# Seven groups of twelve small loads in the load queue of a decode kernel

## The chip, the cores and the metric

The kernel runs on one core of a Trainium2 chip. The metric is the time of one execution in device microseconds; the median of six runs stands for the kernel. A profiled execution gives the trace; it is one execution more, with its own time.

## What is computed

One token passes two pairs of layers, with the same weights in both pairs. The first of a pair is attention over a window of the last 4,096 positions of a cache (32 heads of 192), the second a gated feed-forward layer. Cut to what matters:

```python
def _A_ref(x, k_cache, v_cache, wq, wo):          # x: 1 x 1 x 640
    q = (x @ wq) split into 32 heads of 192
    k, v = the last 4096 positions of k_cache, v_cache   # 32 x 4096 x 192 each
    p = softmax(q k^T * 192 ** -0.5)
    return (p v) @ wo
def _B_ref(x, w1, w3, w2):                         # hidden width 1536
    return (silu(x @ w1) * (x @ w3)) @ w2
x = x + _A_ref(layernorm(x), ...)
x = x + _B_ref(layernorm(x), ...)
x = x + _A_ref(layernorm(x), ...)
x = x + _B_ref(layernorm(x), ...)
```

All arrays are bf16. K and V of the window are about 50 MB each and don't fit on the chip, so nearly all of them are read twice.

## The kernel before, in words

The 32 heads are worked on in four blocks of eight, and a block in four pieces of two heads (`z` = 0 to 3). The K of a piece is one load of 3 MB into all 128 partitions, and so is its V. Layer 0 (the code's name for the first pair) takes the blocks in the order 0, 1, 2, 3 and layer 1 in the order 3, 2, 1, 0; most of block 3 stays on the chip between the layers.

All loads go into one large array `pg`, in which places are given out by hand: seven slots of 3 MB (`slot(0)` to `slot(6)`, counted over all partitions), an area `AUX` for weights, a working area, and `KEPT`, 24 groups of V columns that stay from the end of layer 0 to the first values stage of layer 1. The list of loads, with place and source, is written out ahead by calls of `plan`, `plan_k`, `plan_v` and `plan_cut`. `need(key)` takes the list in order and issues loads on SP's queue (`nc.sync.dma_start`, L111) up to the one that is wanted. So the order on SP's queue is the order of the plan, and only the waits on SP's queue decide when a load is issued: the wait for the readers of what stood in the place before (DVE transposes, PE matmuls), and the wait for a completion semaphore to come free. There are eight of these for the DMA, used in turn, so a load can also wait for the one issued eight before it. One other load, of the token `x` into `xb`, is issued on ACT's queue (L208).

The work on a block: DVE transposes each K in place, four instructions a piece (`k_transpose`, L337); PE computes the scores (`k_scores`, L345; in layer 1's first block two pieces at a time, `pair_scores`, L362); DVE and ACT do the softmax (`softmax_front`, `softmax_back`, L372 to L396); PE multiplies with V (`v_values`, L406); `combine` (L420 to L430) and `times_columns` (L438) put the heads together and multiply with the output weights. The steps of neighbouring blocks are interleaved: the K steps of the next block alternate with the V steps of this one (`steps = "k0 v0 k1 v1 k2 v2 k3 v3"`). In layer 1 the first block goes `v1 v2 v3 k0 v0 k1 k2 k3`, so the values of `v0`, which read `KEPT`, come after a K step. The feed-forward layer follows (`ffn_hidden`, `ffn_out`); the result is stored by SP (L520).

Of the kernel before, what the change touches and what calls it, by code (L numbers as in the profile page):

```python
# [35 lines left out]
KEPT = 14592  # L36
# [27 lines left out]
def kernel(  # L64
# [13 lines left out]
    nc = tc.nc  # L78
# [12 lines left out]
    pg = pages.tile([P, NPG], BF16, name="pg")  # L91

    wq_v = A_wq.rearrange("(p c) n -> p (c n)", c=NCH)
# [9 lines left out]
    def plan(key, at, n, src):  # L103
        queue.append((key, at, n, src))

    def need(key):
        while key not in place:
            k, at, n, src = queue.pop(0)
            for other, (a, m) in live.items():
                assert at + n <= a or a + m <= at, (k, other)  # L110
            nc.sync.dma_start(out=pg[:, at:at + n], in_=src)  # L111
            place[k] = live[k] = (at, n)
        at, n = place[key]
        return pg[:, at:at + n]

    def done(key):
        del live[key]

    def slot(s):
        return SLOT0 + s * SLOT  # L120

    def kv_src(cache, b, z, t0=0, nt=TP):
        off = ((HB * b + 2 * z) * SK + S0 + t0) * DH
        return bass.AP(cache.tensor, cache.offset + off, [[TP * DH, 64], [SK * DH, 2], [1, nt * DH]])

    def plan_k(layer, b, z, s):
        plan(("k", layer, b, z), slot(s), SLOT, kv_src(A_k_cache, b, z))
# [3 lines left out]
    def plan_v(layer, b, z, *places):  # L131
        t = 0
        keys = vkeys[layer, b, z] = []
        for at, nt in places:
            key = ("v", layer, b, z, t)
            if at is None:
                key = ("v", 0, b, z, t)
            else:
                plan(key, at, nt * DH, kv_src(A_v_cache, b, z, t, nt))
            keys.append(key)  # L140
            t += nt

    def cut_v(s):
        at, out_ = slot(s), []
        for nt in CUT_V:
            out_.append((at, nt))
            at += nt * DH
        return out_

    def plan_cut(key, width, cuts, src, at):  # L150
        x = 0
        for i, n in enumerate(cuts):
            plan(key + (i,), at[i] if isinstance(at, tuple) else at + x, n * width, src[:, x:x + n * width])
            x += n * width
# [7 lines left out]
    for i, (n, at) in enumerate(zip(CUT_Q0, (slot(0), slot(1), AUX))):  # L162
        plan(("wq", 0, i), at, n * H * DH, wq_v[:, x:x + n * H * DH])
        x += n * H * DH
    for z in range(NZ):
        plan_k(0, 0, z, 2 + z)
    for (b, ks, vs) in ((0, (6, 1, 3, 5), (0, 2, 4, 6)),
                        (1, (0, 2, 4, 6), (1, 3, 5, 0)),
                        (2, (1, 3, 5, 2), (2, 4, 6, 4))):
        for z in range(NZ):  # L170
            plan_k(0, b + 1, z, ks[z])
            plan_v(0, b, z, (slot(vs[z]), TP))
        plan_cut(("wo", 0, b), D, (12,), wo_v[b], AUX)
# [17 lines left out]
        vkeys[1, 3, z] = list(vkeys[0, 3, z])  # L191
    for (b, ks, vs) in ((2, (4, 1, 5, 6), (0, 3, 2, 4)),
                        (1, (0, 3, 2, 4), (1, 5, 6, 0))):
        for z in range(NZ):
            plan_k(1, b - 1, z, ks[z])
            plan_v(1, b, z, (slot(vs[z]), TP))
        if b == 2:
            plan_cut(("wo", 1, b), D, (12,), wo_v[b], AUX)
    for z, s in enumerate((1, 3, 5)):
        plan_v(1, 0, z, (slot(s), TP))  # L200
    plan_v(1, 0, 3, *cut_v(2))
    plan_cut(("wo", 1, 1), D, (12,), wo_v[1], AUX)
    plan_cut(("wo", 1, 0), D, CUT_WO, wo_v[0], slot(6))
    plan_ffn(1, (slot(4), slot(0), slot(1)))

    need(("wq", 0, 0))
    xb = cst.tile([P, NCH], BF16, name="xb")
    nc.scalar.dma_start(out=xb[:], in_=A_x[0, 0, :].rearrange("(p c) -> p c", c=NCH))  # L208
# [223 lines left out]
    def times_columns(keys, cuts, od, y_ps, first, last):  # L432
        ci = 0
        for key, n in zip(keys, cuts):
            w = need(key)
            for i in range(n):
                for c in range(NCH):
                    nc.tensor.matmul(y_ps[:, c:c + 1], lhsT=w[:, D * i + c:D * i + D:NCH], rhs=od[:, ci:ci + 1],  # L438
                                     start=(first and ci == 0 and c == 0), stop=(last and ci == 11),
                                     skip_group_check=True)  # L440
                ci += 1
            done(key)
# [9 lines left out]
    def ffn_hidden(layer, od):  # L452
        g_ps = ps_a.tile([P, 512], F32, tag="a", name="g_ps")
        c = 0
        for i, n in enumerate(CUT_1[layer]):
            w = need(("w1", layer, i))
            for cl in range(n):
                for j in range(4):
                    nc.tensor.matmul(g_ps[32 * j:32 * j + 32, 0:384], lhsT=xw[:, c, 3:35],
                                     rhs=_ap(w, 0, P, FF * cl + 3 * j, [[12, 128], [1, 3]]),  # L460
                                     start=(c == 0), stop=(c == NCH - 1), tile_position=(0, 32 * j))
                c += 1
            done(("w1", layer, i))
            if i == 0:
                st, rstd = statistics()
                nc.vector.tensor_scalar(out=xn[:], in0=xsq[:, 0:NCH], scalar1=st[:, 0:1], scalar2=rstd[:],
                                        op0=ALU.subtract, op1=ALU.mult)
# [6 lines left out]
        for i, n in enumerate(CUT_3[layer]):  # L474
            w = need(("w3", layer, i))
            for cl in range(n):
                for f in range(12):
                    nc.tensor.matmul(u_ps[:, f:f + 1], lhsT=w[:, FF * cl + f:FF * cl + FF:12],  # L478
                                     rhs=xn[:, c:c + 1], start=(c == 0 and f == 0), stop=(c == NCH - 1),
                                     skip_group_check=True)  # L480
                if c == 0:
                    for k in range(3):
                        nc.tensor.matmul(gt_ps[:, k, :], lhsT=g_sb[:, k:384:3], rhs=selm[:, 0, :], start=True, stop=True)
                    gt = gt_ps[:].rearrange("p k j -> p (k j)")
                    gs = sml.tile([P, 12], F32, tag="gs", name="gs")
                    nc.vector.tensor_scalar_mul(out=gs[:], in0=gt, scalar1=rstd[:])
                    ex = sml.tile([P, 12], F32, tag="ex", name="ex")
                    nc.scalar.activation(out=ex[:], in_=gs[:], func=ACTF.Exp, scale=-1.0)
                    nc.vector.tensor_scalar_add(out=ex[:], in0=ex[:], scalar1=1.0)
                    nc.vector.reciprocal(out=ex[:], in_=ex[:])  # L490
                    nc.vector.tensor_tensor(out=sg[:], in0=gs[:], in1=ex[:], op=ALU.mult)
                c += 1
            done(("w3", layer, i))
# [220 lines left out]
```

## Time and profile before

| | |
|---|---|
| median of 6 runs | 532.5 us (531.7 to 533.56) |
| profiled execution | 532.67 us, span 531.0 us |
| PE busy | 281.7 us, 53% of the span |
| DVE busy | 250.7 us, 47% |
| ACT, POOL busy | 38.1 us, 18.4 us |
| moved by DMA | 221.33 MB, mean 417 GB/s |
| loads issued by SP | 112, from 320 KB to 3 MB |

The span is that of the trace from the first instruction to the last; the execution's time has a little around it. A page of the profile gives busy time by engine, then 40 slices of the span with busy tenths of each engine and of the 16 DMA engines, the DMA queues (q1 is SP's), a chain of waits followed back from the last instruction, and groups of instructions and of DMA issues with their times. A busy share is an average; which engine bounds a stage is read from the slices and from who waits for whom.

### The profile page before, as it was taken

How to read it: one execution, taken by the hardware profiler on the slowest of the kernel's cores; microseconds unless marked ns; L12 is line 12 of the kernel's file. 1: busy time of each engine (PE TensorE's matmuls, PEld its weight loads, DVE VectorE, ACT ScalarE, POOL GpSimd, SP SyncE). 2: the span in 40 equal slices, each digit the busy share in tenths (PEclk: the TensorE clock that was granted, in tenths of full speed). 3: DMA queues.
4: the chain of work that ended last, by engine and by line, in shares of the span. 5: the costliest groups of instructions: out<-in, count | busy, mean ns of one | idle time of the engine just before them, and what ended most of it. 6: DMA issues, size and time to landing. Idle time of an engine off the chain costs nothing.

```text
span 531.0 us, 6794 instructions
## 1 busy us (share of the span) xinstructions
PE 281.7 (53%) x2978; PEld 121.9 (23%) x2978; DVE 250.7 (47%) x304; ACT 38.1 (7%) x93; POOL 18.4 (3%) x71
## 2 busy tenths in 40 slices
PE   1417755550754507836356864944784335845464
PEld 0201111110311103213135432211321122212143
DVE  1269974436484084654011228958465265453010
ACT  0000020000200020002000012002000020002000
POOL 6000000000000000000002040000000000000000
PEclk9998787775678758877665697877777757977555
DMA  8999999999999999999999999999999999999994
GB/s 356 422 434 439 420 439 424 434 424 435 431 425 429 431 433 427 435 421 436 418 383 404 364 399 426 431 433 430 433 429 427 431 430 435 425 433 427 418 409 195
DMA packets 16310, 221.33 MB, mean 417 GB/s; under 512 B 1944, under 2 KB 1944, under 8 KB 7704
## 3 DMA queue, kind: packets, MB, share of 16 engines
q1 hardware_dynamic: 16136, 220.90, 98.5%
q8 instruction: 23, 0.38, 0.3%
q14 instruction: 7, 0.06, 0.0%
q10 hardware_dynamic: 144, 0.00, 0.0%
HBM read 220.89 MB, written 0.00 MB: 416 GB/s over the span
## 4 chain that ended last, share of the span: by engine, by line
DMA 65%; PE 13%; DVE 12%; issue 6%; ACT 2%; SPq 0%; ACTq 0%; DVEq 0%
DMA pg<-in_A_k_cache_dram 47%; DVE pg L337 9%; DMA pg<-in_B_w_dram 7%; DMA pg<-in_A_v_cache_dram 7%; PE s_ps_176 L345 4%; PE s_ps_177 L345 3%; DMA pg<-in_A_wq_dram 2%; PE o_ps L406 2%; DMA xb<-in_A_x_dram 2%; PE y_ps L438 2%; PE s_ps_177 L362 2%; ACT pg L381 1%; DVE pg L384 1%; ACT pg L394 1%; DVE pg L329 0%
## 5 line engine op out<-in xcount | busy, mean ns | idle before, releaser
L337 DVE STREAM_TRANSPOSE pg<-pg 128x1536 uint32<-128x1536 uint32 x112 | 189.0, 1745 | 102.6 <-DMA pg<-in_A_k_cache_dram 102.6
L345 PE MATMUL s_ps_176<-pg 128*32 128x512 bf16 x384 | 87.1, 617 | 59.3 <-DVE pg L337 59.3
L345 PE MATMUL s_ps_177<-pg 128*32 128x512 bf16 x288 | 66.8, 625 | 52.5 <-DVE pg L337 50.1
L345 PEld LDWEIGHTS <-pg 128*32 128x32 bf16 x672 | 41.3, 117 | 209.9 <-issue 196.6
L406 PE MATMUL o_ps<-pg 128*16 128x384 bf16 (+1 forms) x1024 | 74.7, 377 | 25.6 <-DMA pg<-in_A_v_cache_dram 19.8
L406 PEld LDWEIGHTS <-pg 128*16 128x16 bf16 (+1 forms) x1024 | 30.4, 98 | 57.2 <-issue 40.6
L423 PE MATMUL ot_ps<-o_sb,pg 128*128 128x192 bf16 x16 | 3.5, 317 | 64.2 <-ACT o_sb L420 64.2
L438 PE MATMUL y_ps<-otd,pg 128*128 128x1 bf16 x540 | 23.3, 178 | 11.7 <-DVE otd L430 6.8
L438 PEld LDWEIGHTS <-pg 128*128 128x128 bf16 x540 | 23.1, 131 | 13.8 <-issue 8.0
L427 DVE SCALAR_TENSOR_TENSOR om<-ot_ps,rl,dsel 128x192 f32<-128x192 f32 x8 | 3.1, 387 | 37.5 <-PE ot_ps L423 37.5
L381 ACT ACTIVATE pg<-s_ps_176,pg 32x512 bf16<-32x512 f32 x8 | 6.6, 821 | 192.1 <-DVE pg L378 192.0
L381 ACT ACTIVATE pg<-s_ps_177,pg 32x512 bf16<-32x512 f32 (+1 forms) x8 | 6.6, 819 | 169.3 <-DVE pg L378 169.2
L223 POOL MEMSET pg<- 128x128 f32 (+2 forms) x7 | 1.5, 219 | 465.7 <-PE u_ps L478 276.7
L384 DVE STREAM_TRANSPOSE pg<-pg 128x1024 bf16<-128x1024 bf16 x8 | 10.0, 1245 | 15.6 <-ACT pg L381 15.6
L423 PEld LDWEIGHTS <-pg 128*128 128x128 bf16 x16 | 1.6, 100 | 67.8 <-issue 67.8
L415 DVE RECIPROCAL rl<-rl_ps 128x1 f32<-128x1 f32 x8 | 1.3, 169 | 29.7 <-PE rl_ps L413 29.7
L309 PE MATMUL q_ps<-pg,xw 128*32 128x384 bf16 x80 | 7.0, 521 | 15.8 <-DVE xw L219 11.2
L394 ACT COPY pg<-pg 32x256 bf16<-32x256 bf16 (+1 forms) x36 | 14.3, 396 | 7.6 <-DVE pg L384 7.0
L225 POOL TENSOR_SCALAR_AFFINE_SELECT pg<-pg 128x128 f32<-128x128 f32 (+2 forms) x41 | 14.0, 342 | 3.0 <-POOL pg L223 0.3
L362 PE MATMUL s_ps_177<-pg 128*32 128x512 bf16 x96 | 13.4, 634 | 0.0
L309 PEld LDWEIGHTS <-xw 128*32 128x32 bf16 x160 | 6.6, 122 | 25.4 <-issue 12.1
L396 DVE COPY pg<-pg 32x256 bf16<-32x256 bf16 (+1 forms) x36 | 9.8, 272 | 0.6
(100 smaller groups left out, 114.2 us busy)
## 6 DMA issues: line engine op xcount, KB each, us to landing
pg<-in_A_k_cache_dram SPq DMA_DIRECT2D x28, 3072.0 KB, 40.8
pg<-in_A_v_cache_dram SPq DMA_DIRECT2D x25, 3072.0 KB, 38.2
pg<-in_A_wo_dram SPq DMA_DIRECT2D x6, 1920.0 KB, 38.0
pg<-in_A_wq_dram SPq DMA_DIRECT2D x2, 3072.0 KB, 16.8
pg<-in_B_w_dram SPq DMA_DIRECT2D x7, 768.0 KB, 6.6
pg<-in_A_wo_dram SPq DMA_DIRECT2D x6, 640.0 KB, 23.3
pg<-in_A_wq_dram SPq DMA_DIRECT2D x10, 384.0 KB, 5.8
pg<-in_A_wq_dram SPq DMA_DIRECT2D x5, 768.0 KB, 6.1
```

The lines of the kernel that those rows point to most:

```text
L225: nc.gpsimd.affine_select(out=t, in_=t, compare_op=ALU.not_equal, fill=1.0, base=base, pattern=pattern, channel_multiplier=1)
L309: nc.tensor.matmul(q_ps[32 * j:32 * j + 32, 0:384], lhsT=xw[:, c, 3 - c2:35 - c2], rhs=w[:, o:o + 384], start=(first and i == 0), stop=(la ...
L337: nc.vector.transpose(v, v)
L345: nc.tensor.matmul(s_ps[64 * h:64 * h + 32, :], lhsT=wst[:, z, h, it, 4 - 4 * th:36 - 4 * th], rhs=_ap(x, 0, P, 192 * th + 64 * be + par + ...
L362: nc.tensor.matmul(s_ps[32 * q:32 * q + 32, :], lhsT=wst[:, za + i, h, it, 4 - 4 * th:36 - 4 * th], rhs=_ap(x, 0, P, 192 * th + 64 * be + ...
L381: nc.scalar.activation(out=_ap(e, 64 * h, rows, h, [[32, 32], [2, 16]]), in_=s_ps[r, :].rearrange("p (t j) -> p t j", j=16), func=ACTF.Exp ...
L384: nc.vector.transpose(et, e)
L394: nc.scalar.copy(out=dst, in_=src)
L396: nc.vector.tensor_copy(out=dst, in_=src)
L406: nc.tensor.matmul(o_ps[32 * j:32 * j + mw, 0:384], lhsT=ptm[:, po:po + mw], rhs=x[:, 384 * i:384 * i + 384], start=st, stop=(last and u > ...
L423: nc.tensor.matmul(ot_ps[:].rearrange("p q i -> p (q i)"), lhsT=csel[:, par, :, :].rearrange("p h q -> p (h q)"), rhs=o_sb[:, 192 * par:19 ...
L438: nc.tensor.matmul(y_ps[:, c:c + 1], lhsT=w[:, D * i + c:D * i + D:NCH], rhs=od[:, ci:ci + 1], start=(first and ci == 0 and c == 0), stop= ...
```

## The change

A new function `plan_few(i)` puts twelve small loads into the plan: k rows of the query weights, k = 15, 14, 13, 11, 10, 9, 7, 6, 5, 3, 2, 1, each row 256 + 16k elements, into the first k partitions of `pg` at `KEPT`. `need` issues them on SP's queue like other loads (L110 of the changed kernel; the other loads are L114 there), without taking a place for them. Nothing reads what they load. The function is called at seven points of the plan: ahead of the first four K loads; ahead of the loads that belong to blocks 1, 2 and 3 of layer 0; ahead of those of two blocks of layer 1; and ahead of the last V load of layer 1.

```diff
@@ def need(key):
             k, at, n, src = queue.pop(0)
+            if k[0] == "few":
+                nc.sync.dma_start(out=pg[0:k[2], at:at + n], in_=src)
+                continue
             for other, (a, m) in live.items():
                 assert at + n <= a or a + m <= at, (k, other)
             nc.sync.dma_start(out=pg[:, at:at + n], in_=src)
...
+    def plan_few(i):
+        for k in (15, 14, 13, 11, 10, 9, 7, 6, 5, 3, 2, 1):
+            n = 256 + 16 * k
+            plan(("few", i, k), KEPT, n, wq_v[0:k, 0:n])
...
+    plan_few(0)
     for z in range(NZ):
         plan_k(0, 0, z, 2 + z)
     for (b, ks, vs) in ((0, (6, 1, 3, 5), (0, 2, 4, 6)),
                         (1, (0, 2, 4, 6), (1, 3, 5, 0)),
                         (2, (1, 3, 5, 2), (2, 4, 6, 4))):
+        plan_few(1 + b)
         for z in range(NZ):
             plan_k(0, b + 1, z, ks[z])
             plan_v(0, b, z, (slot(vs[z]), TP))
...
     for (b, ks, vs) in ((2, (4, 1, 5, 6), (0, 3, 2, 4)),
                         (1, (0, 3, 2, 4), (1, 5, 6, 0))):
+        plan_few(7 - b)
         for z in range(NZ):
             plan_k(1, b - 1, z, ks[z])
             plan_v(1, b, z, (slot(vs[z]), TP))
...
     for z, s in enumerate((1, 3, 5)):
         plan_v(1, 0, z, (slot(s), TP))
+    plan_few(8)
     plan_v(1, 0, 3, *cut_v(2))
```

## The prediction

> **What bounds the kernel now.** I read first the sliced table of the page, then the queues, then the chain, then the waits of SP's queue, and last short windows at the two ends of the run, where the DMA engines can be seen empty.
>
> In the page, the DMA row and the GB/s row, the queue that carries the loads, and the chain:
>
> ```profile
> DMA  8999999999999999999999999999999999999994
> GB/s 356 422 434 439 420 439 424 434 424 435 431 425 429 431 433 427 435 421 436 418 383 404 364 399 426 431 433 430 433 429 427 431 430 435 425 433 427 418 409 195
> q1 hardware_dynamic: 16136, 220.90, 98.5%
> DMA 65%; PE 13%; DVE 12%; issue 6%; ACT 2%; SPq 0%; ACTq 0%; DVEq 0%
> ```
>
> The 16 DMA engines are busy in every slice but the last; one queue (SP's) fills 98.5% of their span, and PE (53%) and DVE (47%) have room. 220.9 MB have to pass. Time in which the DMA engines stand empty is therefore added to the end, whatever the other engines do meanwhile.
>
> Next, how deep the queue is: the issues with the median time from issue to landing.
>
> ```profile
> pg<-in_A_k_cache_dram SPq DMA_DIRECT2D x28, 3072.0 KB, 40.8
> pg<-in_A_v_cache_dram SPq DMA_DIRECT2D x25, 3072.0 KB, 38.2
> pg<-in_A_wo_dram SPq DMA_DIRECT2D x6, 1920.0 KB, 38.0
> ```
>
> 3 MB at 430 GB/s are 7.3 us, yet they land after 40 us: five or six loads stand ahead of each. Anything issued on this queue lands only after those. SP's own waits say the same from the other side (us in total, times, longest):
>
> ```profile
> SPq L111 <- DVE pg L337: 105.0, 20, 15.4
> SPq L111 <- PE o_ps L406: 73.2, 23, 15.5
> SPq L709 <- DMA out_dram<-pg: 0.9, 1, 0.9
> ```
>
> SP often waits up to 15 us for a free buffer, and it costs nothing because some 40 us of work stand in the rings. The last line is the one place where SP waits for a transfer through empty engines: the store of the result, four rows of 320 B.
>
> Last, the windows at the start (stretch, length, busy of five engines, clock, DMA share, GB/s) and in the middle:
>
> ```profile
> 1.00:1.50 0.50, 0.00 (x0) 0.00 (x0) 0.22 (x3) 0.27 (x1) 0.43 (x3) 1.00 0.00 0
> 1.50:2.00 0.50, 0.00 (x0) 0.00 (x0) 0.00 (x0) 0.50 (x1) 0.36 (x4) 1.00 1.82 442
> 2.00:2.50 0.50, 0.00 (x0) 0.00 (x0) 0.00 (x0) 0.50 (x1) 0.43 (x3) 1.00 0.95 246
> 2.50:3.00 0.50, 0.00 (x0) 0.00 (x0) 0.00 (x0) 0.01 (x1) 0.47 (x1) 1.00 0.30 98
> 3.00:3.50 0.50, 0.00 (x0) 0.00 (x0) 0.00 (x0) 0.00 (x0) 0.47 (x1) 1.00 0.47 197
> 3.50:4.00 0.50, 0.00 (x0) 0.00 (x0) 0.00 (x0) 0.00 (x0) 0.43 (x2) 1.00 1.28 541
> 145.00:222.00 77.00, 38.21 (x350) 14.38 (x347) 44.75 (x40) 3.92 (x9) 0.00 (x0) 0.76 1.01 431
> ```
>
> **What the skill says.** The Trainium skill, page "DMA: Bandwidth & Descriptors", section "Queues, rings and completion order": each engine consumes its ring in order. The 40.8 us landings agree: a load takes its turn. Same page, "Anatomy of one DMA — SWDGE (gpsimd) path": a transfer has a fixed part of about 2.0 us, most of it the receipt of the last write. That is for GpSimd's path; here SP issues, and the trace has the store: issued at 527.92, 0.66 us in SP's queue, then 0.9 us waited, about 1.6 us. Same page, "Why a DMA increments its semaphore by 16 and not by 1": the number of engines is the largest up to 16 that divides the slowest dimension of both sides, so a load of 15 partitions uses 15 engines. No trace here shows that yet, and my sum doesn't hang on it.
>
> **The change, part by part.** It adds 7 groups of 12 small loads on SP's queue: ahead of the first four K loads, behind them, ahead of blocks 2 and 3 of layer 0, of blocks 1 and 0 as next blocks of layer 1, and ahead of the last V load. It removes and reorders nothing: PE, DVE, ACT and POOL keep their instructions.
>
> Bytes: the sum of 2k(256+16k) over the twelve k is 81,664 B per group, 0.57 MB in all, 1.4 us at 417 GB/s. It falls into time counted below, so it is costed at nothing.
>
> Waits: all twelve loads of a group write the same place (KEPT). The compiled order on SP shows what comes of it: each small load but the first waits for the completion of the one ahead of it. Behind it on SP stand all later loads. So per group SP issues the load of 15 partitions, and then nothing until that has landed. In the rings it stands behind everything issued before, and when it lands the engines are empty. From there on, each of the next ten loads (14, 13, 11, 10, 9, 7, 6, 5, 3, 2) is a whole round trip through empty engines. The load of 1 partition is issued after the tenth, and nothing waits for it, so the next large load is issued right behind it.
>
> The round trip: the store took 1.56 us from issue to SP's going on. A load reads from HBM first. At the start of the run the loads are issued at 0.80 and their first bytes appear in the window 1.50 to 2.00, but only some 760 KB pass by 4.00 (half a microsecond times the rates of the five windows). That is the only view of cold reads, and it says that they are slower than warm ones. I add 0.3 us for the read: 1.9 us, an estimate. Below it is bounded by the store's 1.56, less a little (1.5); above by 2.4, if issue and read each take a quarter more.
>
> A group in numbers, as time in which the engines move next to nothing:
> - the engines don't run empty at one moment; at the end of the run the share falls over about two microseconds, and part of that is paid already: 0.7 us (0 to 2)
> - landing of the first small load to SP's going on: 0.3 us
> - ten round trips: 19.0 us (15 to 24)
> - issue of the last small load: 0.4 us
> - restart: from 0.80 to 4.00 the engines moved 0.76 MB where 425 GB/s would have moved 1.36 MB: 1.4 us lost
>
> Sum 21.8 us (17.1 to 28.1). Seven groups: 152.6 us (120 to 197).
>
> What could cover it: nothing in the DMA, which is the bound. In the window 145 to 222 its share was full. The groups do not lie in the stretch from 255 to 307 us where the rate was low (383 to 398 GB/s), so nothing is won back there. The reverse question is whether compute adds to it. After the drain, what still has to run for the landed data is a K transpose (6.8 us), its scores (5.4), a softmax (about 7) and a block of values (2.7), about 22 us if all of it were late; K lands three or four loads ahead of the end of the stage, so it is done before SP goes on, and the buffers are free. Cost nothing. One first small load also waits for PE, since KEPT is read in layer 1 by the values of block 3: in the trace that ends at 339.3, while the K load issued ahead lands at 351.1. The rings cover it; nothing.
>
> The profiled execution took 532.67 us, its span 531.0; the median is 532.5, so the sum may be set on either: 532.5 + 152.6 = 685 us.
>
> **Rivals.**
> - *Serial round trips* (the above): 685 us, with the bounds 652 to 729. Chance 0.88.
> - *Dearer round trips*: odd engine counts make SP's issue slow, or a cold HBM read takes a microsecond more. For: the store's issue took 0.66 us, twice the 0.33 of a 384 KB load. Against: that was counted in its 1.56. At 3.2 us, a group is 34.8 us: 532.5 + 244 = 776 us. It decides if small loads land in over 2.4 us. Chance 0.05.
> - *Cheaper ones*: small reads come back as fast as the first bytes did (0.7 us after issue), 1.2 us in all; a group is 14.8 us: 636 us. Chance 0.04.
> - *Not slower: the chain runs beside the backlog.* If small packets got ahead of the large ones, each round trip would take a few microseconds while the engines stay full. For: a tiny load of x on ACT's queue landed in 10.2 us, ahead of the loads issued with it. The point of decision is the backlog: 12 trips of under 3.3 us fit into the 40 us in the rings. Then only bytes count: 532.5 to 534 us. Against: x has its own queue, and the small loads are on SP's, behind the large ones. Chance 0.02.
> - *The change doesn't do what it says*: the waits don't chain (completed long since), or waiting costs nothing. Time 533 us. Chance 0.01.
>
> **How the numbers follow.** The likeliest gives 685. The range must hold 8 of 10: I take round trips from 1.5 to 2.4 us with the middle values elsewhere: a group is 17.8 to 26.8 us, 657 to 720, and widen to 655 to 725 for the drain. What can be told from no change is about 0.2%, 1.1 us. Slower: the first three cases, 0.97. The last two split, for the most part, into no change (0.02) and a little for a gain (0.01), since a pause in the load stream could at best free another wait.
>
> **What would show it.** Right: the DMA row has seven dips, each of about 22 us; mean rate near 323 GB/s (221.5 MB in 685 us); the small loads land in a median of about 1.6 to 1.9 us, seven of them after 18 to 50; SP's wait of the small loads' line for earlier small loads is the largest in SP's list; the K transposes start near 52 us and not at 30.4. Wrong in size: the median landing of a small load outside 1.5 to 2.4. Wrong altogether: no dips, or dips that are shorter than ten round trips because two small loads are in flight at once.

## The result, and the profile after

The changed kernel takes 665.5 us (median of 10 runs, 663.17 to 666.65) against 532.7 us (20 runs): 1.248 times the time before, 95% interval 1.2464 to 1.2504. That is 132.8 us more, or 19.0 us for each of the seven groups. Its profiled execution took 663.94 us with a span of 662.2 us, 131.2 more than the span before.

From the page of the changed kernel, the sliced DMA rows, the totals and SP's queue:

```profile
DMA  9279189990999909999999999449994499994396
GB/s 374 106 297 429 40 364 436 433 405 6 381 431 429 402 5 404 430 434 422 433 410 392 373 407 425 199 183 435 427 426 177 169 428 438 434 429 200 98 420 271
q1 hardware_dynamic: 17480, 221.47, 80.0%
HBM read 221.46 MB, written 0.00 MB: 334 GB/s over the span
```

The row that was a line of nines has seven holes. A slice is 16.6 us; three of the holes fall on one slice (40, 6 and 5 GB/s), the others across two or three (199 and 183, 177 and 169). Between the holes the rate is what it was, 430 GB/s. The bytes are the same but for 0.57 MB, and the queue's share fell from 98.5% to 80.0%: the time that was added is time in which the engines stand empty.

SP's waits (us in total, times, longest), the largest of its list:

```profile
SPq L110 <- DMA pg<-in_A_wq_dram: 290.9, 77, 42.2
SPq L114 <- PE rl_ps L425: 59.5, 5, 14.5
SPq L110 <- PE o_ps L418: 13.4, 1, 13.4
```

77 waits of a small load for a small load are 7 groups of 11. Seven of them are long, up to 42.2 us: the first small load of a group, landing behind the backlog. The wait for PE, once, 13.4 us, is the group whose place is still being read; the rings covered it, as the hole of that group (slices 26 and 27) is not larger than the others.

One group from near, by the windows of the changed kernel (stretch, length, busy of five engines, clock, DMA share, GB/s):

```profile
146.00:148.00 2.00, 2.00 (x12) 0.64 (x10) 0.00 (x0) 0.00 (x0) 0.00 (x0) 0.50 0.97 415
148.00:151.00 3.00, 3.00 (x22) 0.77 (x20) 0.00 (x0) 0.00 (x0) 0.00 (x0) 0.81 0.20 82
151.00:167.00 16.00, 1.50 (x28) 0.78 (x25) 0.00 (x0) 0.00 (x0) 0.00 (x0) 0.65 0.02 4
167.00:171.00 4.00, 0.00 (x0) 0.00 (x0) 0.00 (x0) 0.00 (x0) 0.00 (x0) 0.50 1.05 387
```

The rings (the loads that are issued and not yet moved) run dry over some two microseconds, which is called the drain below; then 16 us pass at 4 GB/s, then the large loads flow again, which is the restart. PE has 1.5 us of work in those 16, so compute is not what is waited for. What compute there was left ends early in the hole.

The size of a trip stands in the waits of SP in the first group, between 21 and 36 us:

```profile
SPq L110 <- DMA pg<-in_A_wq_dram: 29.0, 10, 18.8
```

Ten waits, the longest of them the drain; the other nine are 10.2 us, 1.13 each. SP's issue of a small load takes 0.27 us (median), and with the step from one to the next the trip is about 1.45 us. I had taken 1.9.

### The profile page after: what moved, and what is told of

It is laid out like the page before. It is cut to its first block, busy times and chain, and to the rows that moved or that the text cites. A ratio compares the mean times of both kernels' runs of the same rounds, so it can differ in the third digit from the quotient of the medians.

```text
span 662.2 us, 6901 instructions
## 1 busy us (share of the span) xinstructions
PE 280.7 (42%) x2978; PEld 123.6 (19%) x2978; DVE 250.8 (38%) x304; ACT 38.3 (6%) x93; POOL 18.5 (3%) x71
## 4 chain that ended last, share of the span: by engine, by line
DMA 68%; PE 12%; DVE 11%; issue 5%; ACT 2%; SPq 1%; ACTq 0%; DVEq 0%
DMA pg<-in_A_wq_dram 49%; DMA pg<-in_A_k_cache_dram 11%; DVE pg L349 8%; DMA pg<-in_B_w_dram 6%; PE s_ps_177 L357 3%; PE s_ps_176 L357 3%; PE y_ps L450 2%; DMA pg<-in_A_v_cache_dram 1%; ACT pg L393 1%; PE s_ps_177 L374 1%; SPq L114 1%; PE o_ps L418 1%; DVE pg L396 1%; DVE pg L341 1%; DVE otd L442 0%
```

## The experiments

The theory: each group costs one drain and restart of the rings, plus ten round trips through empty engines, because SP stands behind each small load in turn. The rivals: the loads are dear in themselves (their odd number of partitions, or what they do in the engines); only the shared place matters; only the trips cost, since the drain is covered.

**One small load a group.**

```diff
-        for k in (15, 14, 13, 11, 10, 9, 7, 6, 5, 3, 2, 1):
+        for k in (15,):
```

> One small load a group (15 partitions) in place of twelve; the rest as in the changed kernel. Theory (the price is serial waits through drained engines): the one small load waits for nothing that is late and nothing waits for it, so the rings stay full: 532 to 535 us. Rival (a small load with an odd number of partitions is dear in itself, by its issue or by what it does to the rings): a twelfth of +133 us or more, 544 us and above.

Measured: 533.5 us against 532.5, ratio 1.0018 (1.0010 to 1.0026). A small load that no later one waits for on SP costs 1.0 us over seven of them. The loads are not dear in themselves.

**Two small loads a group.**

```diff
-        for k in (15, 14, 13, 11, 10, 9, 7, 6, 5, 3, 2, 1):
+        for k in (15, 14):
```

> Two small loads a group (15 and 14 partitions), same place, so that the second waits for the first and SP stands until the rings are empty, but no round trip through empty engines follows. Theory: this leaves the drain and the restart alone. From the trace of the changed kernel: 132.8 us over 7 groups are 19.0 each, of which ten round trips take 14.7 (1.5 for the first, 13.2 for the others); 4.3 remain, 7 x 4.3 = 30: 563 us. As predicted first (drain, wake, issue and restart 2.8 us): 552 us. Rival (only round trips cost, the drain is covered): 533 to 537 us.

Measured: 563.5 us, ratio 1.0578 (1.0562 to 1.0594): 31.0 us, 4.43 a group. SP's wait, and one group's windows:

```profile
SPq L110 <- DMA pg<-in_A_wq_dram: 210.4, 7, 41.2
```
```profile
119.00:121.00 2.00, 2.00 (x12) 0.56 (x10) 0.00 (x0) 0.00 (x0) 0.00 (x0) 0.50 1.04 445
121.00:124.00 3.00, 3.00 (x28) 0.94 (x26) 0.00 (x0) 0.00 (x0) 0.00 (x0) 0.70 0.12 46
124.00:128.00 4.00, 1.22 (x26) 0.58 (x21) 0.00 (x0) 0.00 (x0) 0.00 (x0) 1.00 0.71 243
```

SP waits 210.4 us in seven waits and 31.0 us are lost: all but 4.4 us of each wait is covered by the loads in the rings. Against 430 GB/s, the second window lost 3 x (430 - 46) / 430 = 2.7 us and the third 4 x (430 - 243) / 430 = 1.7 us. SP issues the next large load at 124.09 us, so the first loss is the drain with SP's going on and its issue, and the second is the restart. So one extra load whose issue has to wait for the first is worth 4.4 us, and the ten further ones of the changed kernel 19.0 - 4.4 = 14.5 us, 1.45 each, the same as the trip read from SP's waits.

**Twelve, each at its own place.**

```diff
     def plan_few(i):
+        at = KEPT
         for k in (15, 14, 13, 11, 10, 9, 7, 6, 5, 3, 2, 1):
             n = 256 + 16 * k
-            plan(("few", i, k), KEPT, n, wq_v[0:k, 0:n])
+            plan(("few", i, k), at, n, wq_v[0:k, 0:n])
+            at += n
```

> The same twelve small loads a group, but each at a place of its own inside the kept area, back to back, so that none waits for the one ahead of it because of the place. What stays is that eight completion semaphores are used in turn: each load waits for the one issued eight before it, and twelve in a row make the eighth wait for the last large load. Theory: the chain of ten round trips goes, one drain and restart a group stays with a few more issues of 0.27 us: about 5.3 us a group, 570 us (560 to 580). Rival (only the shared place makes SP wait): 533 to 536 us. Rival (the loads are dear in themselves): 665 us.

Measured: 571.7 us, ratio 1.0737 (1.0716 to 1.0758), 5.6 a group. SP's largest waits:

```profile
SPq L110 <- DMA pg<-in_A_k_cache_dram: 83.3, 12, 7.3
SPq L110 <- DMA pg<-in_A_v_cache_dram: 79.2, 12, 7.4
```

The waits of small loads for small loads are gone from the head of the list; in their place the small loads wait for large ones, up to 7.4 us a time, which is the time of one 3 MB load. That is the turn of the eight completion semaphores. In the trace, every load of this kernel signals the semaphore that the load eight places ahead of it used, and in the third group SP issues its small loads at 92.44, 99.74, 107.04, 114.41 and 121.71 us, each within 0.02 us of the signal of a large load eight places ahead. For the last four of the twelve, the load eight places ahead is a small one of the same group, which lands behind the whole backlog. The chain is gone and with it 94 us; the drain stays, as the DMA row of its page shows with a dip for each group:

```profile
DMA  8798799979999699999999999969998899999696
```

**Six, each at its own place.** As above, with `for k in (15, 14, 13, 11, 10, 9):`.

> Six small loads a group (15, 14, 13, 11, 10, 9), each at a place of its own. With eight semaphores in turn and six in use for small loads, each large load behind the group waits only for one of the large loads ahead of the group or for a small load. Theory: the rings run low to one or two large loads, but not empty; 533 to 541 us. Rival (small loads on this queue cost even where nobody waits for their landing): half of what the twelve apart cost, 552 us.

Measured: 538.3 us, ratio 1.0103 (1.0077 to 1.0128). The DMA row of its page has no hole:

```profile
DMA  8999999999999999999999999999999999999995
```

Half of the small loads cost 5.8 us where twelve cost 39.2. The price follows the point at which the rings run empty, not the number of loads. Most of the 5.8 us are shallow dips that the row of tenths doesn't show, one behind each group. One of them, and the stretch ahead of it:

```profile
118.00:178.00 60.00, 25.68 (x250) 10.49 (x245) 32.40 (x32) 3.92 (x9) 0.00 (x0) 0.72 1.00 428
178.00:182.00 4.00, 4.00 (x36) 1.24 (x34) 0.00 (x0) 0.00 (x0) 0.00 (x0) 0.55 1.06 377
```

Six dips of 4 us at 357 to 394 GB/s and one of 8 us at 348 lose some 4.5 us against 430 GB/s. The rings run low there and not empty.

**The same chain on another queue.** GpSimd issues all 84 small loads, in the same order, to the same place.

```diff
             if k[0] == "few":
-                nc.sync.dma_start(out=pg[0:k[2], at:at + n], in_=src)
+                nc.gpsimd.dma_start(out=pg[0:k[2], at:at + n], in_=src)
                 continue
```

> The same 84 small loads with the same places and the same chain, but issued by GpSimd on its own queue. SP waits for them once only, when the kept area is loaded for the last block of layer 0 (issued at 222 us before), after 48 of them. Theory: the chain runs beside the large loads, whose rings stay full; if a round trip between full rings is under 4.4 us (48 trips between 10 and 222 us), SP loses nothing: 533 to 540 us. If a trip takes as long as the load of x in the kernel before (10.2 us), 48 of them end near 490 us and SP stands for 270: about 800 us. Rival (the loads cost by what they do in the DMA engines): 600 us or more with trips under 4.4.

Measured: 580.7 us, ratio 1.0903 (1.0889 to 1.0917). Neither number was met, because the trip was neither of the two that I had weighed. GpSimd's waits over the run, then SP's between 200 and 275 us, then the windows of that stretch, then PE's wait at the end:

```profile
POOL pg L110 <- DMA pg<-in_A_wq_dram: 413.2, 82, 7.5
```
```profile
SPq L114 <- DMA pg<-in_A_wq_dram: 46.3, 3, 42.5
```
```profile
200.00:245.90 45.90, 29.73 (x284) 11.84 (x285) 23.14 (x22) 1.56 (x4) 3.65 (x7) 0.75 1.00 426
245.90:272.80 26.90, 4.91 (x88) 3.29 (x82) 5.14 (x14) 3.90 (x9) 5.72 (x11) 0.59 0.08 21
```
```profile
PEld z_ps L518 <- POOL pg L237: 23.0, 1, 23.0
```

While the chain ran, the large loads flowed at 426 GB/s: a chain on its own queue does not empty the rings. But a trip beside full rings took some 6.4 us (a wait near 6 and an issue of 0.52 us), so 48 of them were not through when SP had to overwrite the kept area. (Once the rings were empty, GpSimd's trips took 1.9 to 2.2 us.) SP stood for 42.5 us, the rings ran dry, and 26.9 x (1 - 0.08) = 24.7 us were lost. The second half of the chain was not through when GpSimd had to build the identity for the end, and PE waited 23.0 us. Not all of that wait is added time, since large loads were still coming in during its first part. What it added is read from the time behind the last load, here and in the kernel before:

```profile
555.00:578.00 23.00, 8.63 (x173) 6.72 (x173) 2.30 (x11) 1.10 (x4) 3.10 (x7) 0.57 0.01 3
```
```profile
526.00:531.00 5.00, 1.00 (x20) 0.45 (x19) 0.32 (x1) 0.00 (x0) 0.00 (x0) 0.50 0.01 4
```

That is some 18 us. With the 24.7 they are 43 of the 48.2 us measured; the remaining 5 are about what the next kernel costs, in which neither wait is left.

**Half of that chain.** As above, with `for k in (15, 14, 13, 11, 10, 9):`.

> The first six small loads of each group, same place, issued by GpSimd. With all twelve there, a trip between full rings took 6.4 us, the chain outlasted the two points at which other engines wait for it (the load of the kept area at 222 us, the identity that GpSimd builds for the end), and 25 + 23 us were lost. Theory: with half of the trips, 24 x 6.4 = 154 us from 10 us on and 18 x 6.4 = 115 us from 340 us on, both ends are met in time: 532 to 535 us. Rival (a queue of small loads beside the large ones takes bandwidth from them): half of 48, 556 us.

Measured: 537.4 us, ratio 1.0086 (1.0065 to 1.0106). Both long waits are gone, as the theory says, and 4.9 us remain, 2 us above what I had given. The 0.46 MB more that are read would be 1.1 us of them at the mean rate of 417 GB/s. The cause of the rest stays open: the large loads ran at 424 GB/s between 100 and 200 us, where it was 431 before. The rival's 556 us are out, but not that such a queue takes a little of the bandwidth.

**Sixteen partitions throughout, and one.** Two kernels with twelve equal small loads a group, of the same place.

```diff
-        for k in (15, 14, 13, 11, 10, 9, 7, 6, 5, 3, 2, 1):
-            n = 256 + 16 * k
-            plan(("few", i, k), KEPT, n, wq_v[0:k, 0:n])
+        for j in range(12):
+            plan(("few", i, 16), KEPT, 384, wq_v[0:16, 0:384])     # or 1 and wq_v[0:1, 0:384]
```

> Twelve small loads a group of 16 partitions and 384 elements each, same place, in place of the falling row from 15 to 1. In the changed kernel the trips shrink along the row, from about 1.6 us (13 to 10 partitions) to 1.2 (3 and 2). Theory (a trip has a part that grows with the number of partitions): ten trips of 1.6 and 4.3 for drain and restart are 20.3 us a group, 532.5 + 142 = 675 us. Rival (odd numbers of partitions are what makes trips dear): under 655 us. Rival (the number doesn't matter): 665 us.

> Twelve small loads a group of 1 partition and 384 elements each, same place. Theory: ten trips of 1.2 us and 4.3 for drain and restart are 16.3 us a group, 532.5 + 114 = 647 us. Rival (the number of partitions doesn't matter): 665 us. Rival (a load on one engine need only wait for that engine's ring, so the drain is less complete): below 640 us.

Measured: 680.2 us (ratio 1.2778, 1.2739 to 1.2817) with sixteen, 639.5 us (1.1997, 1.1966 to 1.2028) with one. So an odd number is not what makes a trip dear: it grows with the number of partitions. (The bytes of a load grow too, from 768 B to 12 KB, and no run separates the two. At 430 GB/s 12 KB would be 0.03 us, an estimate.) The trip with one partition is again read from SP's waits of the first group, 21 to 36 us:

```profile
SPq L110 <- DMA pg<-in_A_wq_dram: 28.7, 11, 18.8
```

(28.7 - 18.8) / 10 = 0.99 us of waiting and 0.22 of issue, some 1.24 us with the step between. With one partition a group costs 106.9 / 7 = 15.3 us; less ten trips of 1.24 that leaves 2.9 for drain and restart, where two loads of 15 and 14 partitions had shown 4.4. The time fell just under the 640 us of the rival that a load on few engines need not wait for all the rings, and the trace bears this rival out. SP issues the second small load of the third group at 144.82 us, and in the microsecond from 145 on 16 KB still pass, where that small load has 768 B. In the changed kernel SP issues it at 150.93 us, and next to nothing passed in the microsecond from 150 on:

```profile
144.82 0.22 SPq L110 DMA_DIRECT2D pg<-in_A_wq_dram  x1
145.00:146.00 1.00, 1.00 (x12) 0.26 (x10) 0.00 (x0) 0.00 (x0) 0.00 (x0) 1.00 0.05 16
```
```profile
150.00:151.00 1.00, 1.00 (x10) 0.23 (x8) 0.00 (x0) 0.00 (x0) 0.00 (x0) 1.00 0.00 1
```

In five of the seven groups with one partition, packets of large loads still pass for 1.1 to 1.5 us after SP has gone on, and in the other two they end just then. In the changed kernel they have ended 0.5 to 0.6 us before SP goes on, in all seven. That the small load uses one engine is inferred, since the trace does not say which engine moved a packet.

## Why the prediction was right, step by step

*What bounds the kernel*: right. The holes account for the added time; the rate between them is unchanged, and no engine got work that mattered (PE is busy for 280.7 us, before 281.7).

*The chain by the shared place*: right. Eleven waits a group, 77 in all; places of their own took 94 of the 133 us away. What the step left out is that the eight semaphores alone would have drained the rings: I named the place as the only cause of the wait, and twelve loads at twelve places still cost 39 us.

*Ten round trips of 1.9 us*: the term that was too large, 14.5 us a group and not 19.0. I had added 0.3 us to the store's 1.56 for the read from HBM. The runs gave about 1.45 on average over 14 to 2 partitions, even under my lower bound of 1.5; the store of four rows was no lower bound for a load. The difference in issue alone, 0.66 us for the store and 0.27 for the small load, is more than the 0.3 that I had added.

*Drain, wake, last issue and restart, 2.8 us*: too small, 4.4 us by the two-load kernel. Its windows split it: the restart (1.7 us) was near the 1.4 that I read from the start of the run, and the drain with the wake (SP's going on once the small load has landed) and the issue took 2.7 where I had 1.4. Behind the backlog the rings don't end together: in the two-load kernel the busy share of the engines falls to 0.26, 0.08 and 0.01 in three successive microseconds, and SP went on only behind the last of the large loads. Two errors of opposite sign made the sum look better than its terms: 21.8 against 19.0 us. With trips of 1.45 us and my own 2.8 for the rest, a group is 17.3 us and the kernel 654 us, just under the range that I gave; that the result fell inside it is in part luck.

*Covers costed at nothing*: held. The extra wait for PE is there (13.4 us) and covered; PE's work ends early in the hole shown, and the buffers were free behind it: SP issued seven large loads within 5 us.

*Rivals*: trips dearer (over 2.4 us) and trips of 1.2 us are both out on average, though the kernel with one partition reaches 1.24 and single trips of the changed kernel took up to 3.0. That a chain runs beside the backlog was shown possible on another queue, where trips of 6.4 us cost little as long as nobody waits for the end of the chain; on SP's queue the small loads stood behind the large ones, as argued.

*What would show it*: seven dips, yes, of 17 to 21 us by the slices and not of 22; mean rate 334 GB/s for a forecast 323; the first K transpose starts at 46.94 us, for a forecast near 52. Landing times of the small loads are not shown in this profile, so the trips had to be read from SP's waits; in the kernel with sixteen partitions, whose profile has them, the median is 1.6 us and the longest 42.9.

## What to carry to other kernels

In this kernel, which is bound by its loads, a wait on the issuing queue cost nothing until the work in the rings was used up, and from there on it cost in full: with two small loads a group, SP waited 210 us and 31 were lost. So count, for each wait on that queue, what must land before it ends: one load that has to follow a completion on its own queue cost 4.4 us here, each further one 1.45, and a small load that nobody waits for 0.14. Give loads in flight places of their own, and remember that a limited number of completion semaphores makes waits too, even between loads that have nothing to do with each other.

## What was not expected of the hardware

The trip of a small load through empty engines grew with its partitions (or with its bytes, as said above), from 1.24 us with one to about 1.65 with sixteen; SP's issue took 0.22 and 0.31 us of that.

Some single trips were much longer. In the kernel with sixteen partitions, SP's wait between 24.3 and 28 us, and a queue that was busy in the same four microseconds (packets, MB, share of 16 engines):

```profile
SPq L110 <- DMA pg<-in_A_wq_dram: 2.8, 1, 2.8
```
```profile
q8 instruction: 1, 0.02, 2.1%
```

A fetch of 16 KB of instructions passed just then, and the trip was over 3 us instead of 1.6. In the kernel with one partition a like fetch fell between 23.5 and 26.5 us, beside two waits that kept to about 1 us:

```profile
SPq L110 <- DMA pg<-in_A_wq_dram: 1.9, 2, 1.0
```
```profile
q8 instruction: 1, 0.02, 1.9%
```

In the changed kernel and the one with sixteen partitions together, ten fetches fell beside trips; eight of the 140 trips took over 1.8 us (1.9 to 3.2), and each of the eight stood beside a fetch. With one partition five fetches fell beside trips, and none of these took over 1.3 us. That would fit a fetch that runs on one of the sixteen engines, which a load over one partition doesn't use. It is a coincidence in time, not an experiment of its own, and which engine moved the fetch is not shown.
